# Loads of v of units 8 to 23 on GpSimd's queue, and eight output buffers, in a gated linear attention fused with a feed-forward layer

## The chip, the cores and the metric

The kernel runs on one core of one Trainium2 chip. The core has a matrix engine (TensorE, "PE" in the profile, whose loads of stationary weights are listed as "PEld"), VectorE ("DVE"), ScalarE ("ACT"), GpSimd ("POOL") and SyncE ("SP"). Each engine runs its own instructions in their order in the program; engines wait for each other, and for transfers, through semaphores. Transfers between the chip's main memory and the on-chip memory are issued as instructions of an engine's queue (here SP's, at the start also ACT's, and POOL's) and carried out by 16 DMA engines. The metric is the device time of one launch in microseconds (us).

## The reference

A gated linear attention over 768 positions, for 4 batches and 8 heads of 48 columns, and a two-layer feed-forward over its output. Cut to what matters:

```python
f = 1.0 / (1.0 + np.exp(-f_logit))
for t in range(S):
    state = f[:, :, t, :, None] * state + np.einsum('bhd,bhe->bhde', k[:, :, t], v[:, :, t])
    y[:, :, t] = np.einsum('bhd,bhde->bhe', q[:, :, t], state)
...
x = np.ascontiguousarray(attn_out.transpose(0, 2, 1, 3)).reshape(B * S, H * D)
h = x @ w_in
g = np.maximum(0.01 * h, h)
return (g @ w_out).astype(np.float32)
```

All inputs and the output are float32; x has 3,072 rows of 384, the hidden layer is 2,048 wide.

## The kernel before

**Units and pairs.** The positions are cut into 6 chunks of 128. One *unit* is one chunk of one batch with all 8 heads: 24 units, unit u being chunk u // 4 of batch u % 4. Two units in a row, 2m and 2m + 1, make *pair* m, which goes through the feed-forward together (128 + 128 rows).

**Attention of one unit**, from unit 4 on, in the order of its data:
- `load_part` (L171) loads f, k, q or v of a unit, 192 KB each, into one of six float32 buffers of that name (`R_RAW` = 6). One transfer has 128 x 8 pieces of 48 numbers (192 bytes).
- `gate_exp`, `gate_ln` (ACT) make the logarithm of the gate; `gate_pe` sums it along the chunk with a triangular matrix on PE, followed by four narrow products for the decay over the whole chunk; `decay_em`, `decay_a` (ACT) turn the sums into two factors and the chunk's decay.
- `k_scale`, `q_scale` (DVE or POOL) scale k and q by the factors into bfloat16; `cast_v` (DVE or POOL) casts v and so frees its float32 buffer.
- `turn_pe` with `turn_k` and `turn_q`, or, from pair 5 on, `turn2_dma` on SP's queue, turn scaled k and q so that the columns lie on partitions.
- `score1_pe` or `score_pe` (PE), `mask` (DVE), and `mix_pe` (PE) make the unit's output from the scores and from the state before the chunk; `state_pe`, `state_dve`, `state_pool` (with `put_state`) bring the state of the batch up to date.
- `y_out` copies the output into bfloat16 (`xn`), `x_pe` and `x_out` (or `x2_dma`) turn it into `xT`.

**The first four units** (chunk 0 of each batch) are handled together by functions of names that begin with `q_`, with four positions to a partition row; their loads (`first_load`) come first on SP's and ACT's queues.

**Feed-forward.** `up` (L450) is one of eight groups of a pair: six products of 256 columns, then `up_act` (ACT). `down` (L472) is one half of one unit's second layer: eight products of 384 columns; after two halves `put` copies the result into one of four output buffers (`opool`, L48) and `out_dma` (L496) stores it, 192 KB. Pair 2 goes through unit by unit (`up1`, `up_act1`). The weights are loaded by POOL's queue with a cast to bfloat16: `load_w_in` twice, `load_w_out` in four quarters; `down` of half 0 reads the first two quarters of `w_out`, half 1 the other two.

**Fillers.** `idle_pe(n, bank)` issues n products of zeros of 256 columns on PE whose result is not read.

**What sets the order.** The body of the kernel (L501 to L1343) is a list of calls written out by hand, and the schedule is manual: on each engine the instructions stand in the order of the calls. The six POOL loads are those of the weights; every other load from unit 0's v on, every store and every DMA transpose is on SP's queue, in the order of the calls. A load waits for the last reader of its buffer, an output copy for the store that used its buffer before. The last digits of most calls name one of the eight banks of accumulators.

Of the kernel before, what the change touches and what calls it, by code (L numbers as in the profile page):

```python
# [9 lines left out]
FP32 = mybir.dt.float32  # L10
# [6 lines left out]
def kernel(  # L17
# [10 lines left out]
    nc = tc.nc  # L28
# [3 lines left out]
    C = 128  # L32
# [15 lines left out]
    opool = ctx.enter_context(tc.tile_pool(name="opool", bufs=4))  # L48
# [6 lines left out]
    def bank(i):  # L55
        return banks[i][:, :]
# [33 lines left out]

    rep = const.tile([128, 32, 4], BF16, tag="rep")
# [67 lines left out]
    a_ends = ring("a_end", R_AEND, [128, P2], FP32)  # L159
    v_bs = ring("v_b", R_V, [128, H, D], BF16)  # L160
# [10 lines left out]
    def load_part(u, name, src):  # L171
        c, b = units[u]
        t = raws[f"{name}_raw"][u % R_RAW]
        nc.sync.dma_start(out=t, in_=src[b, :, c * C:(c + 1) * C, :].rearrange("h t d -> t h d"))  # L174
        raw.setdefault(u, {})[name] = t
# [147 lines left out]
    def gate_pe(u, bk):  # L323
        c, b = units[u]
        lf = lfs[u % R_LF]
        cs = bank(bk)
        nc.tensor.matmul(cs[:, 0:H * D], ut, lf[:, :, 0:D], start=True, stop=True)
        if c < NCH - 1:
            for p in range(P2):
                nc.tensor.matmul(cs[:, H * D + p:H * D + p + 1], lf[:, 2 * p:2 * p + 2, :], ones_col,  # L330
                                 start=True, stop=True)
# [4 lines left out]
    def decay_a(u, bk):  # L336
        nc.scalar.activation(a_ts[u % R_EM], bank(bk)[:, 0:H * D], AF.Exp, scale=-1.0)  # L337
        if units[u][0] < NCH - 1:
            nc.scalar.activation(a_ends[u % R_AEND], bank(bk)[:, H * D:H * D + P2], AF.Exp, scale=-1.0)

# [155 lines left out]
    def out_dma(u):  # L496
        c, b = units[u]
        nc.sync.dma_start(out=out[b * S + c * C:b * S + (c + 1) * C, :], in_=st[u].pop("osb"))
# [31 lines left out]
    q_turn_pe(khq, 1, 5)  # L530
    q_decay_act(1, 1, aT, -1.0, 2, 1)
    q_k_mul(0, 1, 0, 3)
    q_decay_act(1, 0, aT, -1.0, 4, 0)
    load_part(4, "f", f_logit)
    q_turn_pe(qhq, 1, 6)
    cast_v(G, 0)
    q_k_mul(0, 0, 1, 3)
# [5 lines left out]
    cast_v(G, 1)  # L543
    q_decay_act(1, 0, emT, 1.0, 4, 1)
    q_k_mul(1, 0, 0, 5)
    q_decay_act(1, 1, emT, 1.0, 2, 1)
    q_q_mul(0, 1, 0, 7)
    q_decay_act(1, 1, aT, -1.0, 2, 0)
    q_k_mul(1, 1, 0, 5)
    q_decay_act(0, 1, emT, 1.0, 1, 1)  # L550
    q_q_mul(1, 1, 0, 6)
    idle_pe(11, 0)
# [3 lines left out]
    q_score_pe(1, 0, 2, 1)  # L556
    q_back_out(A, 1, 0)
    q_k_mul(1, 1, 1, 5)
    q_q_mul(0, 0, 1, 7)
    q_back_out(A, 0, 4)  # L560
    q_q_mul(1, 1, 1, 6)
    q_wf_act(1, 0, 1, 1)
    q_score_pe(0, 0, 0, 4)
    q_q_mul(0, 1, 1, 7)
    state_pe(1, 1)
    q_mask(1, 0, 0, 2)
    q_mask_pool(1, 0, 1)
    state_pe(0, 7)
    q_wf_act(0, 0, 1, 4)
    load_part(4, "k", k)  # L570
    q_mask(0, 0, 0, 0)
    q_mask_pool(0, 0, 1)
    q_k_mul(0, 1, 1, 3)
    q_k_mul(1, 0, 1, 5)
    q_mix_pe(0, 2)
    q_score_pe(0, 1, 4, 0)
    q_state_dve(1)
    y_out(A, 0, 2)
    q_back_pe(2, 3)
    q_mix_pe(1, 5)  # L580
    q_wf_act(0, 1, 1, 0)
    q_mask(0, 1, 0, 4)
    q_back_pe(3, 2)
    q_state_pool(1)
    x_pe(0, 1)
    y_out(A, 1, 5)
    q_q_mul(1, 0, 1, 6)
    x_out(A, 0, 1)
    q_mask_pool(0, 1, 1)
    x_pe(1, 0)  # L590
    q_back_out(V, 3, 2)
    q_back_out(A, 2, 3)
    q_score_pe(1, 1, 4, 5)
    q_state_dve(0)
    x_out(A, 1, 0)
    q_wf_act(1, 1, 1, 5)
    q_mask(1, 1, 0, 4)
    q_state_pool(0)
    idle_pe(4, 2)
    up(0, 0, 6)  # L600
    q_mask_pool(1, 1, 1)
    up(0, 1, 1)
    up_act(0, 0, 6)
    up(0, 2, 2)
    load_part(4, "q", q)
    cast_v(V, 2)
    up_act(0, 1, 1)
    load_w_out(0)
    up(0, 3, 3)
    up_act(0, 2, 2)  # L610
# [3 lines left out]
    state_pe(2, 0)  # L614
    q_mix_pe(2, 7)
    up_act(0, 3, 3)
    up(0, 5, 5)
    q_state_dve(2)
    y_out(A, 2, 7)
    load_part(5, "f", f_logit)  # L620
    q_mix_pe(3, 4)
    state_pe(3, 6)
    up_act(0, 5, 5)
    q_state_pool(2)
    up(0, 6, 1)
    y_out(V, 3, 4)
    load_part(5, "k", k)
    gate_exp(4)
    q_state_dve(3)
    x_pe(2, 2)  # L630
    up(0, 7, 3)
    up_act(0, 6, 1)
    x_out(V, 2, 2)
    q_state_pool(3)
    gate_ln(4)
    x_pe(3, 0)
    up(0, 4, 7)
    up_act(0, 7, 3)
    x_out(V, 3, 0)
    load_w_out(2)  # L640
    gate_pe(4, 5)
    up_act(0, 4, 7)
    up(1, 0, 4)
    load_w_out(3)
    decay_em(4, 5)
    up(1, 6, 6)
    decay_a(4, 5)
    k_scale(V, 4)
    up_act(1, 0, 4)
    up(1, 4, 1)  # L650
    up_act(1, 6, 6)
    up(1, 7, 2)
    up_act(1, 4, 1)
    load_part(5, "q", q)
    up(1, 1, 0)
    up_act(1, 7, 2)
    up(1, 3, 3)
    up_act(1, 1, 0)
    q_scale(V, 4)
    down(1, 0, 7)  # L660
    up_act(1, 3, 3)
    turn_pe(4, 5)
    down(0, 0, 4)
    turn_k(A, 4, 5)
    turn_q(V, 4, 5)
    up(1, 5, 6)
    load_part(5, "v", v)
    score1_pe(4, 1, 2)
    up_act(1, 5, 6)
    up(1, 2, 0)  # L670
    mask(4, 0, 1)
    load_part(6, "f", f_logit)
    cast_v(G, 4)
    down(1, 1, 7)
    mask(4, 1, 2)
    up_act(1, 2, 0)
    load_part(6, "k", k)
    gate_exp(5)
    down(0, 1, 4)
    gate_ln(5)  # L680
    put(V, 1, 7)
    load_part(6, "q", q)
    gate_pe(5, 3)
    down(3, 0, 5)
    put(A, 0, 4)
    load_part(6, "v", v)
    decay_em(5, 3)
    decay_a(5, 3)
    k_scale(V, 5)
    load_part(7, "f", f_logit)  # L690
    cast_v(G, 5)
    mix_pe(4, 6)
    q_scale(V, 5)
    down(3, 1, 5)
    y_out(A, 4, 6)
    load_part(7, "k", k)
    gate_exp(6)
    gate_ln(6)
    turn_pe(5, 1)
    put(V, 3, 5)  # L700
    out_dma(1)
    down(2, 0, 0)
    turn_q(A, 5, 1)
    turn_k(V, 5, 1)
    out_dma(0)
    score1_pe(5, 2, 7)
    load_part(7, "q", q)
    gate_pe(6, 4)
    down(2, 1, 0)
    mask(5, 1, 7)  # L710
    load_part(7, "v", v)
    cast_v(G, 6)
    decay_em(6, 4)
    decay_a(6, 4)
    load_part(8, "f", f_logit)
    mask(5, 0, 2)
    k_scale(G, 6)
    gate_exp(7)
    state_pe(5, 3)
    q_scale(V, 6)  # L720
    state_pe(4, 6)
    x_pe(4, 5)
    put(A, 2, 0)
    mix_pe(5, 1)
    state_dve(5)
    gate_ln(7)
    state_pe(6, 7)
    turn_pe(6, 4)
    out_dma(3)
    x_out(A, 4, 5)  # L730
    state_dve(6)
    y_out(A, 5, 1)
    state_pool(5)
    gate_pe(7, 2)
    turn_q(A, 6, 4)
    up1(4, 0, 0)
    load_part(8, "k", k)
    turn_k(V, 6, 4)
    decay_em(7, 2)
    state_dve(4)  # L740
    up1(4, 3, 3)
    load_part(8, "q", q)
    decay_a(7, 2)
    k_scale(G, 7)
    up_act1(4, 0, 0)
    load_part(8, "v", v)
    up1(4, 2, 5)
    q_scale(V, 7)
    up_act1(4, 3, 3)
    state_pool(4)  # L750
    x_pe(5, 1)
    up1(4, 1, 7)
    cast_v(V, 7)
    up_act1(4, 2, 5)
    out_dma(2)
    x_out(V, 5, 1)
    turn_pe(7, 4)
    up_act1(4, 1, 7)
    load_part(9, "f", f_logit)
    up1(5, 1, 6)  # L760
    turn_q(V, 7, 4)
    gate_exp(8)
    load_part(9, "k", k)
    turn_k(V, 7, 4)
    up1(5, 2, 2)
    gate_ln(8)
    load_part(9, "q", q)
    up_act1(5, 1, 6)
    score_pe(3, 0, 3, 1, 5)
    up_act1(5, 2, 2)  # L770
    gate_pe(8, 7)
    up1(5, 0, 4)
    mask(6, 0, 0)
    load_part(9, "v", v)
    decay_em(8, 7)
    decay_a(8, 7)
    mask(6, 1, 3)
    up1(5, 3, 6)
    k_scale(G, 8)
    up_act1(5, 0, 4)  # L780
    load_part(10, "f", f_logit)
    cast_v(V, 8)
    state_pe(7, 2)
    q_scale(V, 8)
    down(4, 0, 0)
    up_act1(5, 3, 6)
    state_dve(7)
    load_part(10, "k", k)
    gate_exp(9)
    mix_pe(6, 7)  # L790
    mask(7, 1, 5)
    load_part(10, "q", q)
    state_pe(8, 3)
    gate_ln(9)
    down(5, 0, 4)
    mask(7, 0, 1)
    state_pool(6)
    y_out(A, 6, 7)
    state_dve(8)
    load_part(10, "v", v)  # L800
    gate_pe(9, 6)
    x_pe(6, 2)
    mix_pe(7, 5)
    load_part(11, "f", f_logit)
    decay_em(9, 6)
    x_out(V, 6, 2)
    turn_pe(8, 1)
    decay_a(9, 6)
    cast_v(V, 9)
    state_pool(7)  # L810
    down(4, 1, 0)
    k_scale(V, 9)
    y_out(A, 7, 5)
    load_part(11, "k", k)
    turn_q(A, 8, 1)
    q_scale(V, 9)
    gate_exp(10)
# [556 lines left out]
```

## Time and profile before

| what | value |
|---|---|
| runs of the kernel before | 181.15 us median of 3 (181.06 to 181.96) |
| the profiled execution, as the runs are timed | 183.12 us |
| its span in the profile | 181.4 us |
| granted clock of PE | 1.0 |
| loads of f, k, q (from unit 4 on), 20 each, on SP's queue, median from issue to landing | 4.3, 4.4, 4.4 us |
| 24 loads of v on SP's queue | 4.6 us |
| six loads of weights on POOL's queue | 10.1 us (w_in), 7.8 us (w_out) |
| moved by all DMA engines | 31.29 MB in 112,581 packets, 105,008 of them under 512 B |

How to read the rows. A page has the busy time of each engine and its share of the span first. A group of instructions is named by line, engine, operation, output <- input, shape, and xcount; then come busy time and the mean of one in ns, and the idle time of the engine before such instructions with what ended it ("<-"). A timeline row has start and length in us, then the same names, xcount for instructions merged into one row, and in brackets the idle time before it. "SPq" is SP's queue: the length is that of the issue, not of the transfer. A chain row has start, length and what ran. A row of a stretch has its bounds and length, the busy time of PE, PEld, DVE, ACT and POOL with the count of instructions, the granted clock, the mean busy share of the 16 DMA engines and what they moved in GB/s; the share can be over 1 where packets overlap on an engine. Lines are those of the kernel before.

### The profile page before, as it was taken

How to read it: one execution, taken by the hardware profiler on the slowest of the kernel's cores; microseconds unless marked ns; L12 is line 12 of the kernel's file. 1: busy time of each engine (PE TensorE's matmuls, PEld its weight loads, DVE VectorE, ACT ScalarE, POOL GpSimd, SP SyncE). 2: the span in 40 equal slices, each digit the busy share in tenths (PEclk: the TensorE clock that was granted, in tenths of full speed). 3: DMA queues.
4: the chain of work that ended last, by engine and by line, in shares of the span. 5: the costliest groups of instructions: out<-in, count | busy, mean ns of one | idle time of the engine just before them, and what ended most of it. 6: DMA issues, size and time to landing. Idle time of an engine off the chain costs nothing.

```text
span 181.4 us, 4726 instructions
## 1 busy us (share of the span) xinstructions
PE 171.7 (95%) x1858; PEld 137.0 (76%) x1858; DVE 89.7 (49%) x198; ACT 123.5 (68%) x268; POOL 53.7 (30%) x109
## 2 busy tenths in 40 slices
PE   4996999999999998999999999999999999999992
PEld 2665799766887678796679987689886696796972
DVE  7449860344969777517586436655372340520000
ACT  2687899464987769795479966669785373571831
POOL 8083652011645107524515213161082310000000
PEclk9999999999999999999999999999999999999999
DMA  4999999979989799997999999999899982220202
GB/s 141 291 213 184 211 183 217 210 143 186 245 178 212 151 192 191 210 188 175 213 217 190 212 158 193 204 213 215 193 191 193 213 197 70 89 43 4 87 1 85
DMA packets 112581, 31.29 MB, mean 173 GB/s; under 512 B 105008, under 2 KB 111280, under 8 KB 112560
## 3 DMA queue, kind: packets, MB, share of 16 engines
q1 hardware_dynamic: 110640, 27.47, 76.2%
q0 software_dynamic: 1376, 3.15, 9.8%
q10 hardware_dynamic: 544, 0.39, 0.8%
q8 instruction: 14, 0.23, 0.5%
q14 instruction: 7, 0.06, 0.1%
HBM read 25.17 MB, written 4.72 MB: 165 GB/s over the span
## 4 chain that ended last, share of the span: by engine, by line
PE 70%; SPq 9%; DMA 8%; DVE 5%; issue 3%; ACT 2%; POOL 1%; DVEq 0%; ACTq 0%
PE ps L474 29%; PE ps L454 27%; SPq L174 5%; SPq L69 3%; DMA v_raw<-in_v_dram 3%; DMA qq<-in_q_dram 2%; DMA f_raw<-in_f_logit_dram 2%; PE ps L465 2%; PE ps L413 2%; PE ps L392 2%; PE ps L410 2%; DVE kTq L258 2%; DVE qTq L258 2%; PE ps L479 1%; PE ps L421 1%
## 5 line engine op out<-in xcount | busy, mean ns | idle before, releaser
L474 PE MATMUL ps<-w_out_b,gT 128*128 128x384 bf16 x368 | 65.5, 326 | 0.0
L454 PE MATMUL ps<-xT,w_in 128*128 128x256 bf16 x528 | 64.5, 273 | 0.0
L459 ACT ACTIVATE gT<-ps 128x512 bf16<-128x512 f32 x88 | 51.2, 607 | 9.8 <-PE ps L454 7.6
L454 PEld LDWEIGHTS <-w_in 128*128 128x128 bf16 x528 | 55.8, 114 | 1.8
L474 PEld LDWEIGHTS <-gT 128*128 128x128 bf16 x368 | 34.6, 98 | 19.9
L403 DVE TENSOR_TENSOR wm<-ps,ut 128x512 bf16<-128x512 f32 x40 | 25.0, 684 | 17.6 <-PE ps L392 15.5
L151 ACT COPY osb<-ps 128x384 f32<-128x384 f32 (+1 forms) x22 | 10.2, 462 | 23.8 <-PE ps L474 20.1
L311 POOL CAST sb<-sf 64x192 bf16<-64x192 f32 x40 | 13.9, 347 | 16.7 <-PE ps L410 11.3
L342 POOL TENSOR_TENSOR kqh<-k_raw,em_t 128x384 bf16<-128x384 f32 x9 | 8.5, 954 | 28.9 <-ACT em_t L334 14.3
L346 DVE TENSOR_TENSOR kqh<-q_raw,a_t 128x384 bf16<-128x384 f32 x13 | 9.1, 703 | 9.5 <-DMA q_raw<-in_q_dram 6.8
L318 ACT ACTIVATE f_raw<-f_raw 128x384 f32<-128x384 f32 x20 | 10.5, 527 | 4.8 <-DMA f_raw<-in_f_logit_dram 4.7
L334 ACT ACTIVATE em_t<-ps 128x384 bf16<-128x384 f32 x20 | 10.0, 498 | 5.4 <-PE ps L330 4.5
L153 POOL CAST v_b<-v_raw 128x384 bf16<-128x384 f32 x9 | 4.5, 505 | 27.5 <-DMA v_raw<-in_v_dram 23.9
L153 DVE CAST v_b<-v_raw 128x384 bf16<-128x384 f32 x15 | 7.3, 484 | 9.3 <-DMA v_raw<-in_v_dram 9.2
L429 DVE TENSOR_TENSOR sf<-sf,ps 64x192 f32<-64x192 f32 x16 | 5.5, 343 | 11.4 <-PE ps L421 5.0
L321 ACT ACTIVATE lf<-f_raw 128x384 bf16<-128x384 f32 x20 | 10.6, 529 | 0.4
L342 DVE TENSOR_TENSOR kqh<-k_raw,em_t 128x384 bf16<-128x384 f32 x11 | 6.8, 620 | 7.0 <-DMA k_raw<-in_k_dram 4.2
L337 ACT ACTIVATE a_t<-ps 128x384 bf16<-128x384 f32 x20 | 9.9, 497 | 0.0
L346 POOL TENSOR_TENSOR kqh<-q_raw,a_t 128x384 bf16<-128x384 f32 x7 | 6.9, 983 | 9.9 <-ACT xT L151 5.1
L435 POOL TENSOR_TENSOR sf<-sf,a_end 128x192 f32<-128x192 f32 x16 | 9.0, 560 | 1.6 <-DVE sf L430 1.1
L153 DVE CAST xn<-ps 128x384 bf16<-128x384 f32 x13 | 7.2, 557 | 4.0 <-PE ps L413 3.2
L145 PE MATMUL ps<-fill 128*128 128x256 bf16 x39 | 7.0, 354 | 1.1 <-DVE uq L129 1.1
(89 smaller groups left out, 198.7 us busy)
## 6 DMA issues: line engine op xcount, KB each, us to landing
v_raw<-in_v_dram SPq DMA_DIRECT2D x24, 192.0 KB, 4.6
out_dram<-osb SPq DMA_DIRECT2D x23, 192.0 KB, 3.3
f_raw<-in_f_logit_dram SPq DMA_DIRECT2D x20, 192.0 KB, 4.3
k_raw<-in_k_dram SPq DMA_DIRECT2D x20, 192.0 KB, 4.4
q_raw<-in_q_dram SPq DMA_DIRECT2D x20, 192.0 KB, 4.4
w_in<-in_moe_w_in_dram POOLq DMA_DIRECT2D x2, 768.0 KB, 10.1
w_out_b<-in_moe_w_out_dram POOLq DMA_DIRECT2D x4, 384.0 KB, 7.8
kq<-in_k_dram SPq DMA_DIRECT2D x4, 192.0 KB, 4.4
```

The source lines that it names most:

```text
L151: eng.copy(out=out, in_=in_)
L153: eng.tensor_copy(out=out, in_=in_)
L311: nc.gpsimd.tensor_copy(out=state_b[b][r, :, e * D:(e + 1) * D], in_=state_f[b][r])
L318: nc.scalar.activation(raw[u]["f"], raw[u]["f"], AF.Exp, scale=-1.0)
L321: nc.scalar.activation(lfs[u % R_LF][:, :, 0:D], raw[u]["f"], AF.Ln, bias=1.0)
L334: nc.scalar.activation(em_ts[u % R_EM], bank(bk)[:, 0:H * D], AF.Exp, scale=1.0)
L342: eng.tensor_mul(khs[u % R_KQS][:, :, 0:D], raw[u]["k"], em_ts[u % R_EM])
L346: eng.tensor_mul(qhs[u % R_KQS][:, :, 0:D], r["q"], a_ts[u % R_EM])
L403: nc.vector.tensor_mul(wms[e][u % R_WM], bank(bk).rearrange("p (i n) -> p i n", i=P2), ut[:, None, :].to_broadcast([128, P2, 128]))
L454: nc.tensor.matmul(bank(bk)[:, i * 256:(i + 1) * 256].rearrange("p (a n) -> p a n", a=2), w_in_p[ff // 8][:, kk, ff // 4 % 2, :, ff % 4], ...
L459: nc.scalar.activation(gTs[m % GBUFS][:, 2 * g:2 * g + 2].rearrange("p f a n -> p (f a n)"), bank(bk), AF.Prelu, alpha=0.01)
L474: nc.tensor.matmul(bank(bk)[:, 0:KD], g_part(u)[:, ff, :], w_out_b[:, ff, :], start=(ff == 0), stop=(ff == NF - 1))
```

## The change

- `load_part` takes the queue as an argument, SP's by default. The calls for v of units 8 to 23 name POOL's. They keep the same buffers and stand elsewhere in the list: those of units 8 and 9 beside the loads of `w_out` (8 and 9 before its last two quarters), 14, 10 and 15 around the first scores of unit 4, 11 behind the cast of unit 5's v, then 12, 16, 17, 13 between the two `state_pool` calls of units 5 and 4 and the `q_scale` of unit 8, and the others in pairs, 18 and 19, 21 and 20, 22 and 23.
- `opool` has eight buffers instead of four, and the stores of the first units stand a little later in SP's order.
- `out_dma` takes a queue too; all calls leave it at SP's. `AEND` is empty, so that `a_rows`, `aend_row` and `aend_dma` make no instruction.
- The whole list of calls is written anew: which engine takes a cast or a scale, which bank a result uses, and where each call stands. In the first stage the fillers before the first `up` become 13 + 1 + 2 + 4 + 10 after `q_q_mul(1, 1, 0, 6)` (before: 11 + 4), and one more stands before `up(3, 7, 6)`; the transposes of units 2 and 3 (`q_back_pe`) stand ahead of `q_mix_pe(0, ...)`. The numbers of calls of each other kind, the transposes on PE and by DMA among them, are the same.

```diff
-    opool = ctx.enter_context(tc.tile_pool(name="opool", bufs=4))
+    opool = ctx.enter_context(tc.tile_pool(name="opool", bufs=8))
...
+    AEND = ()
...
-    def load_part(u, name, src):
+    def load_part(u, name, src, eng=nc.sync):
         c, b = units[u]
         t = raws[f"{name}_raw"][u % R_RAW]
-        nc.sync.dma_start(out=t, in_=src[b, :, c * C:(c + 1) * C, :].rearrange("h t d -> t h d"))
+        eng.dma_start(out=t, in_=src[b, :, c * C:(c + 1) * C, :].rearrange("h t d -> t h d"))
         raw.setdefault(u, {})[name] = t
...
-    def out_dma(u):
+    def out_dma(u, eng=nc.sync):
         c, b = units[u]
-        nc.sync.dma_start(out=out[b * S + c * C:b * S + (c + 1) * C, :], in_=st[u].pop("osb"))
+        eng.dma_start(out=out[b * S + c * C:b * S + (c + 1) * C, :], in_=st[u].pop("osb"))
```

The part of the new list before the first `up`, from the first scores on:

```python
    q_score_pe(1, 0, 2, 1)
    q_k_mul(1, 1, 1, 5)
    q_back_out(A, 1, 0)
    q_q_mul(0, 0, 1, 7)
    q_back_out(A, 0, 4)
    q_q_mul(0, 1, 1, 7)
    q_wf_act(1, 0, 1, 1)
    q_mask(1, 0, 0, 2)
    q_score_pe(0, 0, 0, 7)
    state_pe(1, 4)
    q_k_mul(0, 1, 1, 3)
    state_pe(0, 1)
    q_mask_pool(1, 0, 1)
    q_wf_act(0, 0, 1, 7)
    load_part(4, "k", k)
    q_mask(0, 0, 0, 0)
    idle_pe(1, 2)
    q_score_pe(0, 1, 2, 3)
    q_mask_pool(0, 0, 1)
    q_k_mul(1, 0, 1, 5)
    q_wf_act(0, 1, 1, 3)
    q_state_dve(1)
    idle_pe(2, 7)
    q_back_pe(2, 7)
    q_back_pe(3, 0)
    q_mix_pe(0, 5)
...
    x_pe(0, 4)
    q_score_pe(1, 1, 7, 2)
    q_state_dve(0)
    x_out(A, 0, 4)
    x_pe(1, 5)
    q_wf_act(1, 1, 1, 2)
    q_mask(1, 1, 0, 7)
    q_state_pool(0)
    x_out(A, 1, 5)
    q_mask_pool(1, 1, 1)
    idle_pe(10, 0)
    up(0, 0, 6)
```

And the part around units 5 to 8, with the loads on POOL's queue:

```python
    load_part(11, "v", v, nc.gpsimd)
...
    q_scale(G, 6)
...
    cast_v(V, 6)
...
    k_scale(G, 6)
...
    state_pool(5)
...
    state_pool(4)
...
    load_part(12, "v", v, nc.gpsimd)
...
    load_part(16, "v", v, nc.gpsimd)
...
    cast_v(G, 11)
...
    cast_v(V, 7)
...
    load_part(17, "v", v, nc.gpsimd)
...
    load_part(13, "v", v, nc.gpsimd)
...
    q_scale(G, 8)
...
    turn_pe(8, 5)
...
    gate_pe(9, 7)
```

1334 lines of the change are left out of this document (658 added, 676 removed).

## The prediction

> **What bounds the kernel now.** I read the page's busy shares and chain first, then busy time by stage, then the gaps on TensorE one by one, then the loads.
>
> ```profile
> span 181.4 us, 4726 instructions
> PE 171.7 (95%) x1858; PEld 137.0 (76%) x1858; DVE 89.7 (49%) x198; ACT 123.5 (68%) x268; POOL 53.7 (30%) x109
> PE 70%; SPq 9%; DMA 8%; DVE 5%; issue 3%; ACT 2%; POOL 1%; DVEq 0%; ACTq 0%
> ```
>
> PE is busy for 95% of the span and is 70% of the chain. By stage (after the stretch come its length, then PE busy, PEld, DVE, ACT, POOL, granted clock, DMA share and GB/s):
>
> ```profile
> 7.50:21.40 13.90, 11.95 (x147) 8.52 (x146) 10.08 (x26) 12.01 (x31) 6.89 (x12) 1.00 1.08 206
> 21.40:40.00 18.60, 18.57 (x188) 15.71 (x186) 7.32 (x16) 13.37 (x28) 4.92 (x11) 1.00 1.04 195
> 40.00:54.00 14.00, 13.55 (x203) 10.89 (x201) 9.24 (x20) 11.31 (x28) 5.52 (x10) 1.00 0.96 196
> 54.00:72.00 18.00, 17.04 (x228) 13.92 (x225) 14.46 (x27) 13.65 (x35) 6.21 (x11) 1.00 1.10 190
> 72.00:92.00 20.00, 19.56 (x213) 14.80 (x210) 10.20 (x23) 13.77 (x34) 8.34 (x16) 1.00 0.93 195
> 92.00:110.00 18.00, 18.00 (x194) 15.57 (x194) 10.70 (x23) 15.15 (x34) 5.04 (x9) 1.00 0.99 194
> ...
> 150.00:178.20 28.20, 28.20 (x255) 22.49 (x252) 3.60 (x6) 13.46 (x24) 0.00 (x0) 1.00 0.16 48
> ```
>
> From 21.4 to 178.2 us PE idles 0.03 + 0.45 + 0.96 + 0.44 = 1.88 us, nothing after 92. That is all that better supply can give back once the feed-forward has started, 1.0% of the span. The same rows show the DMA engines full (share 0.93 to 1.10) up to 110 us: the loads are a second bound just under PE. The gaps themselves, on PE's timeline:
>
> ```profile
> 52.02 1.50 PE L465 MATMUL ps<-xT,w_in 128*128 128x128 bf16 x24 [0.45 <-DVE xT L153]
> 62.13 0.34 PE L421 MATMUL ps<-v_b,kqh 128*128 128x96 bf16 x4 [0.30 <-DVE kqh L342]
> 68.14 0.32 PE L327 MATMUL ps<-lf,ut 128*128 128x384 bf16 x1 [0.27 <-ACT lf L321]
> 71.46 0.33 PE L421 MATMUL ps<-v_b,kqh 128*128 128x96 bf16 x4 [0.39 <-DVE v_b L153]
> ```
>
> Each is an operand that came just behind a load: the plan is just in time between 50 and 72 us, and what moves a load there moves PE.
>
> So the time is: start of the first `up`, plus PE's work from there, plus idle time, plus 3.2 us behind PE. The work behind the first `up` is the same in both kernels (the same calls, all added fillers but one stand ahead of it), so two terms decide: **the start** and **the idle time**.
>
> **The start.** The rows of the first stage:
>
> ```profile
> 16.76 1.28 DVE L283 TENSOR_TENSOR wm<-ps,ut 128x512 bf16<-128x512 f32 x2
> 17.95 0.75 DVE L258 TENSOR_TENSOR kTq<-ps,gT 128x256 bf16<-128x256 bf16 x2
> 13.48 1.36 PE L145 MATMUL ps<-fill 128*128 128x256 bf16 x11
> 18.10 0.37 PE L289 MATMUL ps<-v_b,wm 128*128 128x48 bf16 x8 [0.86 <-DVE wm L283]
> 21.24 2.78 PE L454 MATMUL ps<-xT,w_in 128*128 128x256 bf16 x24
> 20.62 0.50 ACT L151 COPY xT<-ps 128x384 bf16<-128x384 bf16 x1
> ```
>
> DVE is the last engine here: `mix` of unit 0 stands waiting for its second mask and starts at 18.10. The new order puts one `kTq` product (0.75/2, about 0.35 us issued back to back) between the two masks, and on PE it puts the transposes of units 2 and 3 ahead of `mix` of unit 0; these need a second such product. So this `mix` starts 2 x 0.35 plus the transposes (about 0.35) later, near 19.15. Behind it on ACT come the `xn` copies of units 0 and 1, `xT` of unit 0, a mask copy that used to stand behind the last `xT`, and `xT` of unit 1 (0.4 to 0.5 us each, as the 0.50 of the row). This ends near 21.8, where before it was 20.62 + 0.50 = 21.12. On PE ten fillers follow the last transpose (before: four), 10 x 1.36/11 = 1.2 us from about 20.9: 22.1 by that count. Start at 22.0 against 21.24: **+0.75 us**; ends: 0 (the ACT copies close up) and +1.2 (all ten fillers bare).
>
> **The loads.** Sixteen of 24 loads of v leave SP's queue, which runs fewer issues, and go to POOL's, which has them far ahead: those of units 8, 9, 14, 10, 15, 11, 12, 16, 17 and 13, in this order, all stand before the `q_scale` of unit 8, which is on POOL too. Each waits there for the cast that frees its buffer, and behind it wait POOL's casts, scales and `state_pool` calls, for which PE's transposes and mixes wait.
>
> ```profile
> L174 SPq DMA_DIRECT2D v_raw<-in_v_dram x24: 432/818/3082, 7.8 to 142.1; - x24
> DMA to landing us min/median/max: 3.6/4.6/14.1
> w_in<-in_moe_w_in_dram POOLq DMA_DIRECT2D x2, 768.0 KB, 10.1
> L190 POOL DMA_DIRECT2D w_in<-in_moe_w_in_dram x2 | 1.7, 862 | 0.0
> L195 POOL DMA_DIRECT2D w_out_b<-in_moe_w_out_dram x4 | 2.2, 549 | 0.0
> q1 hardware_dynamic: 110640, 27.47, 76.2%
> q0 software_dynamic: 1376, 3.15, 9.8%
> ```
>
> SP saves 16 x 0.82 = 13 us of issuing; it is a queue, worth nothing unless it was late. On POOL no load of v was issued before, so its price is bounded by the weights: `w_out` has 128 pieces at 549 ns, `w_in` 384 (128 rows by 3) at 862, so 1.22 ns a piece; v has 1,024 (128 by 8), so 0.55 + 896 x 1.22 ns = 1.64 us. Ends: 0.55 (pieces free) and 2.3 (wholly by piece, 0.862 x 1024/384). Sixteen make 26 us (9 to 37) on an engine busy for 53.7 of 181.4: hidden on average, not where four stand in a row. On the DMA engines a piece of the hardware queue takes 0.762 x 181.4 x 16/110,640 = 20 ns on average over all its sizes; the software queue's average is 207 ns, at over 4 KB a piece, and does not show what 192 bytes cost there. I take a load by the spacing below; lower end 0.92 us, upper end twice the spacing.
>
> The two queues share the engines: the loads of v issued beside `w_in` took up to 14.1 us to land, against 4.6. The Trainium skill (DMA: Bandwidth & Descriptors, Issuing engines are not separate DMA queues) says so too: transfers from all queues run on the same 16 engines and interleave, and another queue saves issue time only. By that rule a load pulled forward delays others; by the opposite reading, a second queue as new bandwidth, the stall of 1.5 us below would be nothing and the sum 1.5 us less.
>
> Now the count at unit 9's gate, the place with most pulled ahead of it:
>
> ```profile
> 53.53 0.43 SPq L174 DMA_DIRECT2D f_raw<-in_f_logit_dram x1
> 61.00 1.30 SPq L174 DMA_DIRECT2D v_raw<-in_v_dram x1
> 69.33 0.93 SPq L498 DMA_DIRECT2D out_dram<-osb x1
> 57.42 0.52 ACT L318 ACTIVATE f_raw<-f_raw 128x384 f32<-128x384 f32 x1 [0.99 <-DMA f_raw<-in_f_logit_dram]
> 58.95 0.33 PE L327 MATMUL ps<-lf,ut 128*128 128x384 bf16 x1
> 32.12 1.30 PE ps L474 x8
> 33.42 0.45 PE ps L355 x8
> 41.09 0.17 PE ps L410 x4
> 41.27 0.20 PE ps L413 x8
> 46.85 0.17 PE ps L444 x3
> 36.00:45.00 9.00, 9.00 (x88) 5.89 (x83) 3.90 (x8) 5.37 (x12) 1.01 (x2) 1.00 0.86 162
> 54.00:62.00 8.00, 7.83 (x108) 5.96 (x104) 6.62 (x14) 5.35 (x15) 3.36 (x7) 1.00 0.89 178
> ```
>
> - When PE wants it: the gate ran at 58.95, 1.53 us after f landed (57.42). The new order has more ahead of it: two halves of `down` (2.60), eight transposes (0.45), one `mix` (0.37), two `x_pe` (0.34): 3.76. With the later start and without the gap at 52.02 that is 58.95 + 3.76 + 0.75 - 0.45 = 63.0, so f is wanted by 61.5.
> - When it lands: eight loads were issued from 61.00 to 69.33, 1.04 us each. Ahead of f9 stood v8; now there stand v8 and five more for certain (9, 14, 10, 15, 11) and up to nine (12, 16, 17, 13 come while POOL gets through them): 5.2 to 9.4 us later. Against it, the DMA engines had room: at 206 GB/s, the rate of the full first stretch, the two slack ones would take 9 x (1 - 162/206) + 8 x (1 - 178/206) = 3.0 us more. Landing at 59.6 to 63.8; I take 63.0, near the upper end, since POOL can issue the last four from about 54 us on.
> - The stall is 1.5 us (ends 0 and 2.3); at twice the spacing, 1.5 + 7 x 1.04 = 9 us.
>
> What leaves: the gaps at 62.13 and 71.46 wait behind v9 and v11, which now come early, and 0.45 and 0.27 give way to the stall. What stays or is new: the 0.44 between 72 and 92, and 0.4 where `down` of unit 0 waits for the last quarter of `w_out`, which now queues behind v8 and v9 on POOL. Idle: 1.5 + 0.44 + 0.4 = 2.3 against 1.88, **+0.45**. Past unit 13 the pulled loads are repaid, and PE had no gap there anyway.
>
> Eight output buffers instead of four and later stores cost nothing: a wait of ACT for a buffer lies beside ACT's 32% of idle time. The new `aend` helpers are never called.
>
> **Sum.** 181.4 + 0.75 + 0.45 = 182.6 us of span, 1.2 more. The profiled execution took 183.12 us by the clock of the runs, 1.7 above its span, and the runs' median is 181.15; on that scale the forecast is 182.4, +0.7%.
>
> **The rivals.**
> 1. *The gaps close.* The second queue fills the room in the DMA engines, no load comes late, 1.4 of the 1.88 us vanish, and the start moves by 0 to 0.75: 179.7 to 180.5. For it: the room of 3.0 us, and later places for the gates in PE's order. Against it: five to nine loads are more than the room. 25%.
> 2. *The software queue is dear.* A piece costs twice on the engines, or POOL needs over 2.3 us for a load: the stall at units 8 and 9 grows to between 3 and 9 us: 184 to 190. It decides from about 1.3 us of engine time a load. For it: no row shows 192-byte pieces on that queue. Against it: 1.22 ns a piece on POOL. 20%. The Trainium skill (SBUF — State Buffer, SBUF: two separate sides) adds a cause: descriptors of a GpSimd load cannot be written while VectorE copies in a two-port mode, and it gives some 620 ns grown to 3,100. By an estimate from that page 16 loads would lose 16 x 2.5 = 40 us of POOL; no row here shows it.
> 3. *POOL blocks itself.* Its loads wait in order for casts of the unit that held the buffer; `q_scale` of unit 8 and two `state_pool` calls stand behind four loads, 4 x 1.64 = 6.6 us. If the `cast_v` of units 6 and 7 come 2 us late, PE waits 2 us more than I count: 184.4. Against it: POOL's 30%. 8%.
> 4. *The queue does not matter*, the start closes up and one stall replaces another: 181.2 to 181.8. 7%.
>
> **How the numbers follow.** My own case has 40%, with 181.4 to 183.5 as its range. A change under 0.5% (0.9 us) can't be told from none here: faster is below 180.25, slower above 182.05. Rival 1 gives 0.20 to faster and 0.05 to the same; rival 4 gives 0.07, my case 0.13 to the same and 0.27 to slower; rivals 2 and 3 give 0.28 to slower: 0.20, 0.25, 0.55. The range 180.0 to 187.5 leaves out the dearest end of rival 2 and the best of rival 1.
>
> **What would show it.** Right: the first `up` near 22.0; PE idle before the transposes or the gate of units 8 and 9, released by a q or f load; the GpSimd loads near 1.6 us. Wrong: GpSimd loads of 3 us or more, or landing 8 us after issue (rival 2); PE released by POOL's work (rival 3); no gap over 0.5 us behind 21 us (rival 1).

## The result, and the profile after

| kernel | time, us | against the kernel before | profiled span |
|---|---|---|---|
| before, four runs beside the new one | 181.56 median (181.06 to 183.28) | 1 | 181.4 |
| new | 189.52 median (187.12 to 193.35) | 1.0319 [1.0253, 1.0384] | 189.3 |
| forecast | 182.4 (180.0 to 187.5) | 1.007 | 182.6 |

The ratio leaves out the two of the four runs of the new kernel that lie over 1.5% above its fastest; the profiled run is one of them, and its span is 3 to 4 us longer than those of the two others (185.4 and 186.4). So the account of 7.9 us below is that of one execution; the ratio stands for about 5.8 us. The new kernel is slower, as forecast, but by 3.2% and not by 0.7%.

The page of the new kernel (busy shares, chain, two of its DMA queues, the group of GpSimd's loads):

```profile
PE 175.5 (93%) x1874; PEld 139.2 (74%) x1874; DVE 88.0 (46%) x196; ACT 123.6 (65%) x268; POOL 70.9 (37%) x127
q1 hardware_dynamic: 94000, 24.32, 68.3%
q0 software_dynamic: 2400, 6.29, 16.8%
PE 56%; DMA 21%; SPq 14%; ACT 3%; issue 2%; DVE 1%; POOL 1%; ACTq 0%; DVEq 0%; POOLq 0%
L178 POOL DMA_DIRECT2D v_raw<-in_v_dram x16 | 14.4, 904 | 14.2 <-DVE v_b L154 13.4
v_raw<-in_v_dram POOLq DMA_DIRECT2D x16, 192.0 KB, 6.3
```

PE fell from 70% to 56% of the chain, and transfers rose from 8% to 21%. A load costs GpSimd 0.90 us. Its cost on the DMA engines can be estimated from the rows of the software queue (the time of its packets): 0.168 x 189.3 - 0.098 x 181.4 = 14.0 us of 16 engines, 0.88 us a load. The count of packets says how it does that: 2,400 - 1,376 = 1,024 more for 16 loads, 64 a load, four for each of 16 engines, where SP's queue has 1,040 for such a load ((110,640 - 94,000) / 16). SP's queue makes a packet of every 192-byte piece; GpSimd's packs the pieces, (6.29 - 3.15) MB / 1,024 = 3.1 KB a packet on average. The two pages count 2,070 packets of 2 KB or more against 1,301 before, so about 48 of the 64 carry the load, at some 4 KB each.

The same stretches as before (length; busy PE, PEld, DVE, ACT, POOL; granted clock; DMA share; GB/s):

```profile
21.40:40.00 18.60, 16.07 (x167) 14.70 (x167) 7.32 (x18) 12.68 (x27) 8.17 (x15) 1.00 1.02 195
40.00:54.00 14.00, 14.00 (x170) 10.04 (x168) 6.62 (x12) 7.93 (x20) 4.51 (x7) 1.00 1.14 201
54.00:72.00 18.00, 17.65 (x230) 14.61 (x229) 12.70 (x30) 14.90 (x34) 10.63 (x19) 1.00 0.99 185
72.00:92.00 20.00, 18.68 (x203) 14.26 (x202) 10.88 (x23) 14.80 (x35) 11.13 (x16) 1.00 1.05 206
92.00:110.00 18.00, 15.70 (x179) 12.17 (x178) 9.20 (x20) 10.87 (x26) 9.22 (x15) 0.91 1.12 152
150.00:186.05 36.05, 36.05 (x336) 29.31 (x333) 5.48 (x10) 18.46 (x33) 1.53 (x2) 1.00 0.24 62
```

Length less busy PE gives the idle time: 2.53 + 0 + 0.35 + 1.32 + 2.30 = 6.50 us, against 1.88. 5.86 us of it stand in three gaps on PE's timeline; the first row here is the first `up`:

```profile
22.58 2.13 PE L465 MATMUL ps<-xT,w_in 128*128 128x256 bf16 x18
37.98 0.40 PE L366 MATMUL ps<-ident,kqh 128*128 128x128 bf16 x4 [2.53 <-DVE kqh L357]
79.45 0.34 PE L432 MATMUL ps<-v_b,kqh 128*128 128x96 bf16 x4 [1.03 <-DVE kqh L353]
100.44 0.62 PE L403 MATMUL ps<-kqT 64*128 64x128 bf16 x16 [2.30 <-DMA kqT<-kqh]
```

The sum: 1.34 us of later start, 4.62 us more idle time, and (1 - 0.991) x 189.3 = 1.7 us at a lower clock make 7.7 of the 7.9 us between the spans. The work behind the first `up` is the same: 186.05 - 22.58 - 6.50 - 1.7 = 155.3 us, before 178.20 - 21.24 - 1.88 = 155.1.

**The gap at unit 4.** The transposes of unit 4 wait for its scaled q, and that for the load of q4. SP's queue, by the tile of that load, in the new kernel and then in the one before:

```profile
L178 SPq DMA_DIRECT2D q_raw<-in_q_dram x1: 680/680/680, 22.8 to 22.8; - x1
DMA to landing us min/median/max: 14.5/14.5/14.5
```

```profile
L174 SPq DMA_DIRECT2D q_raw<-in_q_dram x1: 940/940/940, 23.4 to 23.4; - x1
DMA to landing us min/median/max: 8.6/8.6/8.6
```

Beside it run the four `w_out` loads and now v8 and v9. What the engines did from 32 to 35 us, by queue (packets, MB, share):

```profile
q0 software_dynamic: 207, 0.57, 96.1%
q1 hardware_dynamic: 210, 0.04, 12.4%
```

While GpSimd's queue has work nearly all the time, the two queues get the same number of packets (207 and 210), but a GpSimd packet took 0.961 x 3 us x 16 / 207 = 223 ns and one of SP's 28 ns: SP's queue got an eighth of the engines' time. Before, from 32 to 34 us, the four `w_out` loads did the same (141 and 142 packets, shares 97.7% and 11.7%); now GpSimd's share is over 90% all the way from 26 to 35 us. The Trainium skill (DMA: Bandwidth & Descriptors, Queues, rings and completion order) has this rule: each engine takes turns between the queues it has work for, a whole packet a turn. The trace agrees, with 207 to 210. As each 192-byte piece is a packet on SP's queue here, equal turns make very unequal shares.

**The gap at pair 6.** The scores of pair 6 wait for their DMA transpose. SP's queue by the tile it writes:

```profile
L376 SPq DMA_TRANSPOSE kqT<-kqh x1: 3941/3941/3941, 89.1 to 89.1; - x1
DMA to landing us min/median/max: 11.3/11.3/11.3
```

Before, the seven transposes of k and q took 4.2 to 6.9 us. Here the load of v20 was issued 0.33 us behind the transpose, and both landed near 100 us. Behind this gap PE ran at half clock (same columns as the stretches):

```profile
98.00:100.00 2.00, 0.14 (x5) 0.05 (x2) 0.08 (x1) 1.37 (x4) 0.00 (x0) 1.00 1.24 96
100.00:102.00 2.00, 1.56 (x22) 1.22 (x23) 0.84 (x2) 0.00 (x0) 0.49 (x1) 0.79 1.39 198
102.00:104.00 2.00, 2.00 (x11) 1.45 (x10) 1.32 (x3) 0.91 (x2) 0.68 (x2) 0.50 0.53 94
104.00:106.00 2.00, 2.00 (x28) 1.75 (x27) 0.75 (x3) 1.72 (x4) 1.99 (x3) 0.86 0.90 177
```

That is (0.21 + 0.50 + 0.14) x 2 = 1.7 us, all that the clock cost.

**The gap at 79.45.** It ends with a scaled k on DVE. That waited for ACT's `decay_em`, and ACT had stood 1.76 us until a load of f landed (its `gate_exp` runs at 77.90). So all three gaps go back to a transfer.

### The profile page after: what moved, and what is told of

It reads as the page before. It is cut to its first block, busy times and chain, and to the rows that moved or that the text cites. A ratio compares the mean times of both kernels' runs of the same rounds, so it can differ in the third digit from the quotient of the medians.

```text
span 189.3 us, 4768 instructions
## 1 busy us (share of the span) xinstructions
PE 175.5 (93%) x1874; PEld 139.2 (74%) x1874; DVE 88.0 (46%) x196; ACT 123.6 (65%) x268; POOL 70.9 (37%) x127
## 3 DMA queue, kind: packets, MB, share of 16 engines
q1 hardware_dynamic: 94000, 24.32, 68.3%
q0 software_dynamic: 2400, 6.29, 16.8%
## 4 chain that ended last, share of the span: by engine, by line
PE 56%; DMA 21%; SPq 14%; ACT 3%; issue 2%; DVE 1%; POOL 1%; ACTq 0%; DVEq 0%; POOLq 0%
PE ps L485 24%; PE ps L465 21%; SPq L178 13%; DMA q_raw<-in_q_dram 10%; DMA kqT<-kqh 6%; DMA fq<-in_f_logit_dram 3%; DMA f_raw<-in_f_logit_dram 2%; PE ps L403 2%; PE ps L476 1%; PE ps L424 1%; PE ps L490 1%; PE ps L421 1%; PE ps L331 1%; PE ps L432 1%; PE ps L366 1%
## 5 line engine op out<-in xcount | busy, mean ns | idle before, releaser
L465 PE MATMUL ps<-xT,w_in 128*128 128x256 bf16 x528 | 65.3, 277 | 0.0
L470 ACT ACTIVATE gT<-ps 128x512 bf16<-128x512 f32 x88 | 51.8, 601 | 18.0 <-PE ps L465 15.6
L465 PEld LDWEIGHTS <-w_in 128*128 128x128 bf16 x528 | 56.9, 115 | 2.8 <-issue 0.3
L315 POOL CAST sb<-sf 64x192 bf16<-64x192 f32 x40 | 15.2, 379 | 17.3 <-PE ps L421 14.1
L178 POOL DMA_DIRECT2D v_raw<-in_v_dram x16 | 14.4, 904 | 14.2 <-DVE v_b L154 13.4
L353 DVE TENSOR_TENSOR kqh<-k_raw,em_t 128x384 bf16<-128x384 f32 x11 | 7.3, 664 | 12.7 <-ACT em_t L338 11.2
L357 DVE TENSOR_TENSOR kqh<-q_raw,a_t 128x384 bf16<-128x384 f32 x12 | 7.2, 600 | 12.7 <-DMA q_raw<-in_q_dram 9.0
L154 DVE CAST xn<-ps 128x384 bf16<-128x384 f32 x14 | 7.8, 556 | 10.5 <-PE ps L424 8.2
L146 PE MATMUL ps<-fill 128*128 128x256 bf16 x55 | 9.7, 336 | 1.2 <-DVE uq L130 1.1
L146 PEld LDWEIGHTS <-fill 128*128 128x128 bf16 x55 | 6.4, 120 | 2.9 <-issue 1.2
```

Of the source, the lines that this page charges most:

```text
L146: nc.tensor.matmul(bank(bk)[:, 0:256], fill[:, 0:128], fill[:, 0:256], start=True, stop=True)
L178: eng.dma_start(out=t, in_=src[b, :, c * C:(c + 1) * C, :].rearrange("h t d -> t h d"))
L315: nc.gpsimd.tensor_copy(out=state_b[b][r, :, e * D:(e + 1) * D], in_=state_f[b][r])
L353: eng.tensor_mul(khs[u % R_KQS][:, :, 0:D], raw[u]["k"], em_ts[u % R_EM])
L357: eng.tensor_mul(qhs[u % R_KQS][:, :, 0:D], r["q"], a_ts[u % R_EM])
L465: nc.tensor.matmul(bank(bk)[:, i * 256:(i + 1) * 256].rearrange("p (a n) -> p a n", a=2), w_in_p[ff // 8][:, kk, ff // 4 % 2, :, ff % 4], ...
```

## The experiments

**1 to 3. Mending the two places.** The loads of units 8, 9, 14 and 15 were moved behind the crowd around `w_out` (first), those of 21 and 20 away from the transpose (second), and both (third).

```diff
# first
-    load_part(8, "v", v, nc.gpsimd)
-    load_part(9, "v", v, nc.gpsimd)
...
     load_part(10, "v", v, nc.gpsimd)
+    load_part(8, "v", v, nc.gpsimd)
+    load_part(9, "v", v, nc.gpsimd)
...
     x_out(A, 5, 2)
+    load_part(14, "v", v, nc.gpsimd)
+    load_part(15, "v", v, nc.gpsimd)
# second
     k_scale(G, 15)
+    load_part(21, "v", v, nc.gpsimd)
+    load_part(20, "v", v, nc.gpsimd)
```

> The new kernel with the four GpSimd loads of v of units 8, 9, 14 and 15 taken from the stretch of the w_out loads: 8 and 9 go behind the load of v10 (which waits for the cast of v4), their casts behind those of units 6 and 10, 14 and 15 behind these. Theory (turns by packet): while GpSimd's queue has packets of 4 KB, SP's pieces of 192 bytes get one turn for each and starve. Without v8 and v9 the weights' queue has pauses again, q4 lands at 32 to 33 us instead of 37.3, the gap of 2.5 us at unit 4's transposes falls under 0.5, and the time falls by 1.5 to 2.5 us from the new kernel's 187.1 to 188.1 to about 185.5. Rival (engine time only: a load costs its own 0.88 us, no more): q4 lands near 37.3 - 2 x 0.88 = 35.5, a gap of 0.8 to 1.5 stays, and the time falls by 1 us or less.

> The new kernel with the GpSimd loads of v of units 21 and 20 put behind the k_scale of unit 15, so that they don't run beside the DMA transpose of pair 6. Theory: that transpose lands 6 to 7 us after its issue begins (11.3 in the new kernel), as the others do; the gap of 2.3 us before the scores of pair 6 falls under 0.3 and the 3.4 us at half clock behind it go, so the time falls by 2.5 to 4 us, to 183.5 to 185. Rival (the transpose is late because SP's queue is late, whatever runs beside it): it still takes 9 us or more, and the time falls by under 1 us.

> Both edits at once. Theory: the gaps are independent, both go, 4 to 6 us in all: 181.5 to 183.5, that is 0.2 to 1.3% over the kernel before, the rest being the later start (1.3 us) and small gaps. Rival (the loads are a bound of their own, and a gap that is closed comes back later): 185 or more.

Measured: first, 184.85 us once and 188.15 to 189.91 in the five other runs, without a ratio; second, 187.28 us, 1.0303 [1.0256, 1.035]; third, 186.62 us, 1.026 [1.0215, 1.0305]. The times that the three theories gave (about 185.5, 183.5 to 185, 181.5 to 183.5) were not reached, but for that one run of the first. q4 in the first, by the same view as above:

```profile
L178 SPq DMA_DIRECT2D q_raw<-in_q_dram x1: 977/977/977, 23.9 to 23.9; - x1
DMA to landing us min/median/max: 8.3/8.3/8.3
```

8.3 us is a landing at 32.2, where the rival by engine time alone had 35.5. The gap before unit 4's transposes is gone; 0.73 us stand at the scores behind them. The other profiles agree: q4 took 7.6 to 8.8 us in the five new-list kernels in which no v load of GpSimd's queue stands near it (runs 1, 3, 6, 9 and 10), and 12.9 to 14.9 in the three in which v8 and v9 do (the new kernel, runs 2 and 5). In run 6 the same two loads stand at the same places on SP's queue, and q4 took 8.8. So the late q4 is shown to come from these loads on GpSimd's queue, as the turns have it. The transpose of pair 6 in the second:

```profile
L376 SPq DMA_TRANSPOSE kqT<-kqh x1: 2937/2937/2937, 87.9 to 87.9; - x1
DMA to landing us min/median/max: 4.6/4.6/4.6
```

4.6 us for 11.3, and the gap there is gone. So both loads do what was said, but the time did not follow. For pair 6 the 2.30 us may not be typical of the new kernel: in the first kernel the same transpose, with v20 issued 0.30 us behind it, took 8.9 us, and PE did not wait there. Two stretches of the second kernel, and the same two of the third:

```profile
21.40:40.00 18.60, 16.18 (x157) 14.13 (x155) 6.84 (x16) 12.51 (x25) 8.59 (x14) 0.92 1.10 207
54.00:72.00 18.00, 17.77 (x237) 14.92 (x235) 12.82 (x29) 14.86 (x35) 11.20 (x20) 1.00 1.07 185
```

```profile
21.40:40.00 18.60, 18.13 (x182) 15.53 (x180) 6.81 (x16) 12.83 (x26) 7.00 (x14) 1.00 1.08 206
54.00:72.00 18.00, 14.93 (x202) 12.74 (x200) 11.58 (x26) 13.84 (x33) 10.38 (x17) 1.00 0.98 182
```

Closing the gap at unit 4 (2.42 us and the half clock behind it) came with 3.07 us of idle time between 54 and 72, and the spans are 184.3 and 184.5. In the first kernel PE idles 6.9 us in all, 2.72 of them between 54 and 72, and the span is 187.7. Two of the new gaps of the third:

```profile
65.47 0.32 PE L331 MATMUL ps<-lf,ut 128*128 128x384 bf16 x1 [1.18 <-ACT lf L325]
69.08 0.34 PE L432 MATMUL ps<-v_b,kqh 128*128 128x96 bf16 x4 [1.11 <-DVE kqh L353]
```

The first is a gate, the kind of stall that was forecast: ACT had stood 0.95 us for the load of f, which took 8.5 us. The rival of the third run has the time (185 or more) and the sign right: gaps come back later.

**4. The old list with all 16 loads on GpSimd's queue.** Only the queue is changed, at the old places in the list.

```diff
-    load_part(8, "v", v)
+    load_part(8, "v", v, nc.gpsimd)
...
-    load_part(23, "v", v)
+    load_part(23, "v", v, nc.gpsimd)
```

> The kernel before with nothing changed but the queue of the loads of v of units 8 to 23: GpSimd's, at their old places in the list. Theory (what hurts is GpSimd packets beside urgent loads on SP's queue): GpSimd has few instructions, so the loads come as early as their buffers allow, often beside urgent f, k and q loads; each holds SP's queue back for about its own 0.9 us at seven turns in eight. Without the crowd around w_out I expect gaps of 1 to 3 us in all and no late first up: 182 to 184.5. Rival A (the queue is worse by itself): as slow as the new kernel, 186 to 188. Rival B (the queue does not matter, only the new list): 181.0 to 181.8.

Measured: 183.06 us, 1.0052 [1.0017, 1.0086], inside the theory's range; both rivals fall. One of twelve runs took 190.6 us, and that is the profiled one, so the small gaps behind the 0.5% were not seen. Its PE timeline and the tile of its transpose:

```profile
85.43 1.03 PE L392 MATMUL ps<-kqT 64*128 64x128 bf16 x16 [6.12 <-DMA kqT<-kqh]
```

```profile
L365 SPq DMA_TRANSPOSE kqT<-kqh x1: 3107/3107/3107, 72.9 to 72.9; - x1
DMA to landing us min/median/max: 12.5/12.5/12.5
```

v13 was issued at 72.98, 0.12 us behind the transpose. Over the 14 profiled kernels there are 98 such transposes. In eight of them a GpSimd load was issued 0.1 to 0.7 us behind the transpose, and these took 6.4 to 12.5 us, 8.3 in the middle; the 90 others took 4.2 to 7.8, and two of them more than 6.9. Two of the eight stayed under 6.9.

**5. Another way to mend unit 4.** Added to the second kernel; here the load of v14, into the buffer of v8, stands ahead of the cast of v8, so that this cast waits for v14 and unit 8 is computed with unit 14's v: this kernel leaves out v8.

```diff
     load_w_out(2)
+    load_part(8, "v", v, nc.gpsimd)
+    load_part(9, "v", v, nc.gpsimd)
...
     turn_q(V, 4, 5)
+    cast_v(V, 8)
```

> The run with v20 and v21 later, and v8 and v9 moved by two places only: behind the last w_out quarter on GpSimd's queue, the cast of v8 behind unit 4's turn_q. The earlier edit moved v14 and v15 too and paid at 55 to 83 us. Theory (turns by packet): the weights' queue has its pauses back, q4 lands at 32 to 33 us, the gap of 2.4 us at unit 4 and the half clock behind it go, and since all else stays in its order no gap comes back: 182 to 184. Rival (the loads are a bound of their own): gaps of 1.5 us or more come up between 45 and 75 us, 185 to 187.

Measured: 186.67 us, 1.025 [1.0214, 1.0285]. Because of that cast it doesn't test what it was made for. PE idles much as in the other versions: gaps of 1.11 and 1.20 us near unit 4, 1.55 at 79 us, and a span of 185.0.

**6. The new list without the second queue.** The 16 loads stay where the new list has them, on SP's queue.

```diff
-    load_part(8, "v", v, nc.gpsimd)
+    load_part(8, "v", v)
...
```

> The new list with the 16 loads of v on SP's queue at the same places: same order, no second queue. v14, v15 and v10 now hold SP's queue while they wait for casts. Theory (order and queue both count): q4, in front of v8 on one queue, lands at 32 to 33 us, and the DMA transposes take 4 to 7 us, as nothing of GpSimd's runs beside them; but f, k and q of units 6 to 10 stand behind up to nine pulled loads and behind SP's waits, gaps of 2 to 5 us between 40 and 75: 184 to 187. Rival A (the queue alone is at fault, the order is good): 181 to 183. Rival B (the new list is at fault whatever the queue): 186 to 189, with the gap at unit 4 still there.

Measured: 186.39 us, 1.0245 [1.0221, 1.027], and five runs between 186.26 and 186.83 where the new kernel's four spread from 187.1 to 193.4. Rival A, by which the queue alone is at fault, falls. The time lies in the theory's range and in rival B's (186 to 189, the new list at fault whatever the queue), so it does not part these two. PE idles 1.53 us at unit 4's scores and 1.75 before a `down` at 73.8, in all 4.4 us; the theory had gaps of 2 to 5 between 40 and 75. Followed back, both gaps end at a load: the first at v8, whose cast stands ahead of the copy of unit 4's turned q on DVE and waited until it landed at 36.6, the second at a load of f, for which ACT stood 1.64 us before it could go on to the `up_act` that this `down` reads.

**7, 8 and 11. Parts of the change in the old list.** The loads of v8 to v12 alone on GpSimd's queue; eight output buffers alone; both.

```diff
-    opool = ctx.enter_context(tc.tile_pool(name="opool", bufs=4))
+    opool = ctx.enter_context(tc.tile_pool(name="opool", bufs=8))
...
-    load_part(12, "v", v)
+    load_part(12, "v", v, nc.gpsimd)
```

> The kernel before with only the loads of v of units 8 to 12 on GpSimd's queue, at their old places: behind the weights and before the first DMA transpose. Theory: what hurt the old list on that queue was a load beside the DMA transpose of pair 5 (12.5 us instead of 4 to 7); without one, every transpose takes under 7 us, no run stands out by several us, and the gaps of 0.30 and 0.39 us behind v9 and v11 go: 180.8 to 181.9, up to 0.5% faster than before. Rival (a second queue costs by itself, wherever it runs): 0.5% or more slower, as when all 16 were on it.

> The kernel before with eight output buffers and nothing else. Theory: within 0.3% of before (181.4 to 182.4); the buffers free nothing that PE waits for. Rival (more buffers let output copies run ahead and change ACT's order of waits): 0.5% or more either way.

> The two edits of the old list that were each a little faster, together: v of units 8 to 12 on GpSimd's queue, eight output buffers. Theory: both take small waits away before the first DMA transpose and add up: 0.5% faster than before (0.3 to 0.8%). Rival (they close the same gaps): 0.2 to 0.4%.

Measured: 0.9963 [0.9937, 0.9989], 0.9976 [0.9949, 1.0002] and 0.9969 [0.9948, 0.999]. The five loads are worth 0.4%; the buffers can't be told from nothing. The two together gained 0.3%, no more than the loads alone, which is nearer to the rival; but the intervals overlap, so whether the two add up isn't shown. No transpose of the seventh kernel took over 6.8 us. The stretch that lost 0.96 us before, in the eleventh:

```profile
54.00:72.00 18.00, 18.00 (x250) 15.00 (x247) 15.64 (x30) 14.64 (x35) 9.75 (x17) 1.00 1.09 185
```

The gaps behind v9 and v11 are gone. By their ratios runs 7 and 11 are the fastest kernels here, by 0.3 to 0.4%, little but more than the noise.

**9 and 10. The new list with no load pulled ahead.** Each v from unit 8 on stands right behind q of its unit, on SP's queue (9) or GpSimd's (10), and its cast behind the unit's last scale.

```diff
     load_part(8, "q", q)
+    load_part(8, "v", v)
...
     k_scale(V, 8)
+    cast_v(V, 8)
```

> The new list with no load pulled ahead and no second queue: v of each unit from 8 on goes onto SP's queue right behind its q, its cast behind the unit's last scale. Everything else of the new list stays. Theory (the pulled loads are the loss, the rest of the list is about as good as the old one but starts 0.5 us later): no gap over 0.7 us, q4 at 32 to 33 us, 182 to 183.5. Rival (the new order of the computing calls is worse by itself): 185 to 187 as with the pulled loads on SP's queue (186.4), with gaps again near unit 4's scores or near 74 us.

> The same order, with the 16 loads on GpSimd's queue. Theory: as in the old list, the queue by itself costs about 0.5% (1 us) over the same order on SP's queue, and a load issued within 0.4 us behind a DMA transpose makes that transpose take 7 to 12 us in some runs: 0 to 1.5 us over the run on SP's queue, some runs several us more. Rival (the second queue is the loss wherever the loads stand): 186 to 189, as the new kernel.

Measured: 187.19 us, 1.0276 [1.0243, 1.0309], and 186.08 us, 1.0232 [1.0202, 1.0263]. The theory (182 to 183.5) falls in the ninth: without any pulled load the new list is as slow. The tenth's, 0 to 1.5 us over the ninth, missed too: it is 1.1 us below. Some of the ninth's gaps:

```profile
24.98 0.33 PE L432 MATMUL ps<-v_b,kqh 128*128 128x96 bf16 x4 [1.07 <-DVE v_b L154]
63.45 0.33 PE L432 MATMUL ps<-v_b,kqh 128*128 128x96 bf16 x4 [0.56 <-DVE v_b L154]
76.57 0.33 PE L432 MATMUL ps<-v_b,kqh 128*128 128x96 bf16 x4 [0.55 <-POOL v_b L154]
127.57 0.32 PE L331 MATMUL ps<-lf,ut 128*128 128x384 bf16 x1 [1.21 <-ACT lf L325]
132.47 0.62 PE L403 MATMUL ps<-kqT 64*128 64x128 bf16 x16 [0.88 <-DMA kqT<-kqh]
```

The first is a wait for a load of v that was issued at 9.3 us, in the first stage; two kernels of the old list have it too (0.42 and 0.60 us in runs 8 and 12). The gaps behind a cast of v (0.56 and 0.55) may be those of casts put too late here, so the run doesn't weigh the new order of the computing calls cleanly. The 1.21 us at a gate and the 0.88 at a transpose are not of that kind: before the gate ACT stood 1.89 us for a load of f that took no longer than most (4.0 us), so it was issued too late for where its gate stands. That the tenth is no slower than the ninth says again that the queue by itself is not the loss.

**12. A load meant to start beside a transpose.** The eleventh kernel, with the q scale of unit 11 on GpSimd and the load of v13 behind it.

```diff
-    q_scale(V, 11)
+    q_scale(G, 11)
+    load_part(13, "v", v, nc.gpsimd)
```

> The kernel of the run before this one with one load more on GpSimd's queue, that of v13, placed to start together with the DMA transpose of pair 5: the q_scale of unit 11, for which the transpose waits, goes to GpSimd, and the load stands right behind it. Theory (a GpSimd load that starts with a transpose and that transpose hold each other up): the transpose takes 8 to 12.5 us instead of about 5, PE waits 2 to 6 us before the scores of pair 5, the time rises by 2 to 6 us. Rival (a transpose is late only where the other loads crowd too): the transpose takes under 7 us and the time rises by under 1 us, the price of a scale on GpSimd.

Measured: 181.95 us, 1.0005 [0.9979, 1.0031]; the transpose took 6.0 us. It missed its aim: the load was issued at 71.56, and SP, still issuing a load of k, got to the transpose at 72.74, so the load went 1.2 us ahead and not behind. This leaves the collision known by the eight cases and by the second run, in which the load was taken away; its cause inside the engines is open.

## Why the prediction was right and wrong

**Right: the formula, the sign and the start.** Start, PE's work, idle time and 3.2 us make up every span; the work came out at 153.8 to 155.6 us in all 14 profiles, once the time lost to a lower clock behind the start is taken off. The start was forecast as 21.24 + 0.75 = 22.0. In the profiles of the new list it lies between 21.57 and 22.58, about 21.9 in the middle; the one beside the result is the latest. The old list has 21.14 to 21.37, and once 22.02 (run 7), where PE ran at half clock from 18.7 us on. So the shift is about 0.65 us, no more than one execution can differ by.

**Luck: the range.** 3.2% over the 181.15 us of the forecast's scale is 186.9, just inside 180.0 to 187.5 (the four runs' own median, 189.52, is not). That end of the range was there for rival 2, a dear software queue, which is not what happened; the forecast's own case ended at 183.5.

**The small prices.** GpSimd issues a load in 0.90 us, within the ends (0.55 to 2.3) but not near the 1.64 that was to be a sign. The engines need 0.88 us for it by the estimate above and 0.93 by runs 9 and 10, at the lower end of 0.92. The prediction's 207 ns for a packet of the software queue belong to 3.15 MB / 1,376 = 2.3 KB on the page, not to over 4. Eight buffers are worth nothing that can be measured. The gaps behind v9 and v11 left, as said. `down` did not wait for the last `w_out` quarter, for which 0.4 us had been put down.

**Wrong: idle time, +0.45 forecast, +4.62 measured in the profile, and the clock.** The 1.5 us at unit 9's gate, the main term, did not come: PE has no gap over 0.3 us there. Three steps failed.
- *A load was counted by its own 1.04 us.* "The two queues share the engines" was right, but it took fair sharing by load. By packet, SP's queue gets an eighth as long as GpSimd's has work. So v8 and v9 cost q4 not two loads' time but nearly six us (14.5 against 8.6 us to landing), and the stall stood at unit 4, where none was looked for.
- *"Past unit 13 the pulled loads are repaid, and PE had no gap there anyway."* The pulling goes on to v23, and 2.30 us were lost at pair 6, through a transpose that the forecast never set beside a GpSimd load. The 1.7 us at half clock stand behind this gap. The Trainium skill (TensorE: Matmul & The Clock Gate, What's actually happening) has the clock halved when PE was idle for a window of about 3.4 us; the traces show 3.4 us at half speed behind this gap of 2.30 and behind the second run's of 2.42, both shorter than that window, and none behind the one of 2.53 at unit 4. So they don't agree with that length, and what sets the clock back stays open here.
- *The list was taken to cost nothing beyond its start.* It was said that two terms decide because the calls are the same. But five versions of the new list, with v early or late, on either queue, have spans of 184.3, 184.5, 184.5, 185.3 and 184.3 (runs 2, 3, 6, 9, 10), run 1 has 187.7, and four of the old list other than the run of 190.6 have 179.5 to 180.5. From the first `up` on PE idles 2.8 to 5.2 us in the five and 0.6 to 1.4 in the four: the gaps move, and most of the loss stays. Without the second queue the new list is still 2.45% slower (run 6), and the second queue in the old list costs 0.5% (run 4), so the list is the larger part of the 3.2%.

Why the list loses this time I can argue, not prove. The DMA engines are about full in either list, as one long stretch shows, before and then in the second run:

```profile
7.50:140.00 132.50, 128.68 (x1478) 103.00 (x1477) 77.26 (x162) 101.12 (x231) 47.60 (x90) 1.00 1.04 197
```

```profile
7.50:140.00 132.50, 128.75 (x1472) 103.11 (x1473) 74.99 (x159) 98.23 (x225) 64.19 (x108) 0.99 1.06 202
```

With a share of 1.04 and 1.06 a load that comes earlier makes another later, and a PE that is sooner at its next gate waits there. By this argument a list fits if it asks for its operands no sooner than the 197 to 202 GB/s of these stretches can bring them; PE idles 0.6 to 1.9 us in the old one, 2.8 to 5.2 in the new one. The gaps that were followed back (the new kernel's three, run 3's at a gate, both of run 6 and two of run 9) do end at a transfer, four times at a load of f for which ACT stood. Others, as run 9's behind casts, end at the order of the work. Which of the list's calls ask too soon was not tried, nor unit 4 mended without another change beside it.

**The rivals.** Rival 2 (184 to 190) has the time but not the mechanism: a load costs GpSimd and the engines 0.9 us each, no more than forecast, and the queue is hard on its neighbour. Its sign, a landing over 8 us after issue, did come up (6.3 us in the middle, 10.6 at most), so that sign does not tell a dear queue from a crowded one. Rival 3: GpSimd did wait 13.4 us for casts, but none of PE's three gaps ends with its work. Rival 4 is nearest for the queue by itself, +0.5% in the old list. Rival 1 is what the five loads do in the old list.

## What to carry to other kernels

Before putting loads on a second queue, look at what a packet is on each: here, while the second queue was full, its packets of 2 to 4 KB left an eighth of the engines' time to the queue with 192-byte pieces, so the loads that are wanted first must not run beside it. When the DMA engines are full, add up the idle time of every gap, not of the mended one: here a load pulled ahead was paid for by another. Try one part of a change in the old order first; here five loads and nothing else gained 0.4%.

## What the runs showed of the hardware

- GpSimd's time to issue a load grows far less than the count of its pieces: 549 ns for 128, 862 for 384, 904 for 1,024.
- On the engines a load of v is no cheaper on the second queue. From run 9 to run 10, where only the queue changes, the packets of SP's queue fall from 74.6% of 185.3 us to 68.3% of 184.3, 0.77 us a load, and those of GpSimd's rise from 9.8% to 17.9%, 0.93 us a load.
- A load of 192 KB in 192-byte pieces is 1,040 packets on SP's queue and 64 on GpSimd's. Where both queues have work they get packets in equal number (207 and 210), so time goes by the size of the packet.
- A DMA transpose with a GpSimd load issued 0.1 to 0.7 us behind it was late in six of the eight cases above (7.1 to 12.5 us, against 4.2 to 6.9 in 88 of 90 others), and once PE waited 6.12 us for it. Which of the two holds up the other isn't shown.
